# Lower prices for VectorE's operations in the planner that hands out the steps of two transforms between matmuls

## The chip, the cores and the metric

One Trainium2 chip, one of its cores. The metric is the device time of one execution in microseconds (us). Engines: TensorE (PE), VectorE (DVE), ScalarE (ACT), GpSimd (POOL) and SyncE (SP, which only issues DMAs here).

## The reference

```python
def _A_ref(x, w_r, w_i):
    X = jnp.fft.rfft2(x, axes=(-2, -1))
    X = X * (w_r + 1j * w_i)
    return jnp.fft.irfft2(X, s=(S, D), axes=(-2, -1))

def _B_ref(x, w1, w2):
    h = _silu(jnp.einsum("bsd,df->bsf", x, w1))
    return jnp.einsum("bsf,fd->bsd", h, w2)

xn = _layernorm(x)
return x + _A_ref(xn, w_r, w_i) * _silu(_B_ref(xn, w1, w2))
```

x is 2048 rows of 1024, w1 is 1024 by 3584, w2 is 3584 by 1024, w_r and w_i are 2048 by 513; all are float32. So there are two big matmuls with a SiLU between them (the dense part), and beside them a two-dimensional transform, a product with a filter and the inverse transform (the spectral part), joined in the last line.

## The kernel before, in words

Every float32 operand of a matmul is split into a high and a low half of 16 bits, and each product is made by three matmuls (high by high, high by low, low by high). `high` (L251, on ACT) and `low` (L254, on DVE) make the halves.

The dense part sets the order. The first matmul, `mm1` (L456), has 112 tiles of 24 matmuls of 512 columns: four blocks c of 512 rows by 28 blocks f of 128 hidden columns. The second, `mm2` (L539 to L541), is done with seven products m of sums and differences in place of eight; for each of them there are eight tiles j, and each tile is done in two halves of 21 matmuls of 512 columns. I call such a half of 21 matmuls a **half-tile**. `acc` adds a tile's result to the running sums (L582 to L609), and `w2_gen` prepares the weights of the next product, one block per call (L251, L254, tile `w`). The last sums go through `final` and `finish_out` (L623, L624) to the output.

The spectral part runs in the gaps, as generators in the list `bg`, in this order: layer norm (`ln_gen`), the forward transform along the rows (`fd_gen`, four blocks), the transform along the columns with the filter (`f_gen`), a small exact treatment of the edge of the spectrum (`edge_gen`), and the inverse (`i_gen`, four blocks c in the order 1, 3, 0, 2). Each `next` of a generator is one step: it issues some instructions on all engines and yields. All engines work their instructions off in the order of issue, so the order of the steps is the order on each engine.

`f_gen` has 16 turns u. A turn is four steps:

- step 1: `high_z(u-1)` (ACT L981), then on DVE `xb`, `xd` (L1004, L1005) and four operations of `radix4` (L238 to L241): 6 DVE operations, 2048 elements per partition in all.
- step 2: `low_z(u-1)` (L986) and the products with the filter (L1019, L1020): 3 operations, 3072 elements. Every fourth turn it also sets up the stores of `zq` to DRAM (`zd`, L990); `zq` has one buffer, so the next block of four waits for these stores.
- step 3: `mat(u+1)` on PE, 36 matmuls (L954 to L956), then on DVE L1032, L1033, L1036, L1037: 4 operations, 2048 elements.
- step 4: a copy on ACT (L975), the operations on `Z` (L1055): 8 on DVE with 896 elements, 4 on POOL.

After the last turn, `edge_gen` copies edge values on POOL (L1078 to L1081, behind POOL's share of the last `Z`), multiplies them by permutations on PE (`eps`, L1085 to L1087), and calculates on POOL.

In each block, `i_gen` has four matmul groups `iu` (L1204 or L1212) with the DVE work `post` (L1220 and on) and `split` (L1283, L1284), then four groups `mat2` (`id`, L1294) with the DVE work `bfly` (L1307 to L1341). `fx`, `iu`, `id` and `eps` take their PSUM tiles from one pool of two buffers; the result of group p leaves its buffer at L1308 of `bfly(p)`.

The planner is `work` (L1447). `meter` is called with every instruction as it is issued and keeps two clocks: for PE 0.4215e-3 us per column of output, for DVE a fixed price per operation and a price per element of the largest operand per partition. `work` is called once after each tile of `mm1` (but the first four) and after each half-tile of `mm2`. It gives one step to the weights (`wq`), lifts the DVE clock to at least the PE clock less 1.0, and then hands out up to three steps of `bg`, as long as the DVE clock is at most 1.0 (`LEAD`) ahead of the PE clock; a step that yields `PAUSE` ends it. In the last four tiles of `mm1` nothing is handed out (`hold`). 15 tiles before the end of `mm1` what is left of the forward transform is finished at once, and `f_gen` begins behind it.

Of the kernel before, what the change touches and what calls it, by code (L numbers as in the profile page):

```python
# [127 lines left out]
def spectral_ffn(ctx, tc, x, w_r, w_i, w1, w2, ca, kc, ci, tw, pm, out):  # L128
# [80 lines left out]

    clock = {"pe": 0.0, "dve": 0.0}  # L210

    COST = {"DVE": ("dve", 0.12, 1.05e-3), "PE": ("pe", 0.0, 0.4215e-3)}

    def meter(inst):

        name, fixed, each = COST.get(str(inst.engine).split(".")[-1], (None, 0, 0))
        rows = [math.prod(n for _, n in a.ap[1:]) for a in (*inst.outs, *(inst.ins if name == "dve" else ())) if hasattr(a, "bass_ap")]
# [1407 lines left out]
```

## Time and profile before

| | us |
|---|---|
| median of 3 runs (lowest, highest) | 1235.48 (1234.14, 1237.49) |
| the profiled execution's own time | 1235.84 |
| its span in the trace | 1234.1 |
| PE busy in the span | 1220.7 |
| DVE busy in the span | 999.0 |
| first `mm1` matmul to last `mm1` matmul | 19.3 to 636.3 |
| `mm2` | 636.5 to 1229.2 |

The span is the time from the first to the last instruction in the trace; 1.74 us of the execution lie outside it. A busy time is the time in which at least one instruction of the engine was under way. Matmuls overlap, so the busy time of PE does not say that it was at its peak; the distance between the starts of matmuls does. Idle time is put down to what ended it.

### The profile page before, as it was taken

What the parts mean: (1) busy time and instruction counts of PE and PEld (TensorE: products, weight loads), DVE (VectorE), ACT (ScalarE), POOL (GpSimd) and SP (SyncE); (2) the same over time, 40 slices, a digit from 0 to 9 for tenths busy, and PEclk for the clock granted to TensorE, in tenths of its full rate; (3) what the DMA queues carried; (4) which work ended last, traced back from release to release, by engine and by line L of the source; (5) the groups of instructions that cost most, each with busy time, mean ns of one, the idle gap of its engine ahead of it and who ended that gap; (6) DMA issues with size and microseconds to landing.
All of it is one profiled execution on the core that took longest, in us unless ns stands there. A gap on an engine that the chain in (4) does not pass through costs nothing.

```text
span 1234.1 us, 19097 instructions
## 1 busy us (share of the span) xinstructions
PE 1220.7 (99%) x7033; PEld 625.2 (51%) x7033; DVE 999.0 (81%) x1970; ACT 467.6 (38%) x614; POOL 117.3 (10%) x245
## 2 busy tenths in 40 slices
PE   8999999999999999999999999999999999999998
PEld 5545445444544454445545555554455555555545
DVE  7687988899798898896969899985186678798886
ACT  4865344333554565444433222122032222243212
POOL 2330000001000000010001121114111111000000
PEclk9999999999999999999999999999999999999999
DMA  7487476655758898759898999997989999998576
GB/s 253 134 172 187 135 224 201 185 152 161 223 172 237 276 283 242 217 177 279 207 283 224 283 259 198 276 256 246 293 207 278 286 289 331 315 332 325 200 261 260
DMA packets 271102, 293.67 MB, mean 238 GB/s; under 512 B 40096, under 2 KB 198816, under 8 KB 270624
## 3 DMA queue, kind: packets, MB, share of 16 engines
q1 hardware_dynamic: 250992, 233.66, 65.7%
q10 hardware_dynamic: 15984, 51.45, 12.0%
q0 software_dynamic: 4032, 7.34, 3.5%
q8 instruction: 55, 0.90, 0.3%
q14 instruction: 39, 0.32, 0.1%
HBM read 185.95 MB, written 102.25 MB: 234 GB/s over the span
## 4 chain that ended last, share of the span: by engine, by line
PE 75%; DVE 11%; DMA 9%; issue 2%; ACT 1%; SPq 0%; POOL 0%; DVEq 0%; ACTq 0%; POOLq 0%
PE pa L456 45%; PE pb L539 8%; PE pb L541 8%; PE pb L540 8%; DVE Z L1055 2%; DMA wq<-in_A_w_i_dram 2%; DMA sd<-s 2%; PE id L1294 2%; DMA zd<-zq 1%; DMA ht<-hd_sum_d 1%; DVE T L1020 1%; DVE w L254 1%; PE iu L1204 1%; ACT xp L709 1%; PE iu L1212 1%
## 5 line engine op out<-in xcount | busy, mean ns | idle before, releaser
L456 PE MATMUL pa<-xnT,w 128*128 128x512 f16 x2688 | 585.2, 379 | 1.1 <-ACT w L251 0.7
L456 PEld LDWEIGHTS <-w 128*128 128x128 f16 x2688 | 262.2, 98 | 311.6 <-DVE w L254 1.3
L539 PE MATMUL pb<-w,ht 128*128 128x512 f16 (+2 forms) x812 | 300.4, 372 | 0.0
L540 PE MATMUL pb<-w,ht 128*128 128x512 f16 (+2 forms) x812 | 300.4, 372 | 0.0
L541 PE MATMUL pb<-w,ht 128*128 128x512 f16 (+2 forms) x812 | 300.3, 372 | 0.0
L541 PEld LDWEIGHTS <-ht 128*128 128x128 f16 x812 | 79.4, 98 | 91.0
L539 PEld LDWEIGHTS <-ht 128*128 128x128 f16 x812 | 79.5, 98 | 86.7
L540 PEld LDWEIGHTS <-ht 128*128 128x128 f16 x812 | 79.4, 98 | 86.7
L465 ACT ACTIVATE h<-pa,s 128x512 f32<-128x512 f32 x112 | 75.5, 678 | 122.9 <-PE pa L456 111.0
L251 ACT ACTIVATE w<-jr,sc 128x512 f16<-128x512 f32 x98 | 68.1, 713 | 77.8 <-PE pb L541 22.1
L254 DVE SCALAR_TENSOR_TENSOR w<-jr,sc,w 128x512 f16<-128x512 f32 x98 | 71.1, 744 | 2.1 <-ACT w L251 2.1
L254 DVE SCALAR_TENSOR_TENSOR hoone<-h,hs,hoone 128x2048 f16<-128x2048 f32 x28 | 65.6, 2344 | 7.9 <-ACT hoone L251 7.9
L251 ACT ACTIVATE hoone<-h,hs 128x2048 f16<-128x2048 f32 x28 | 56.0, 1998 | 36.5 <-DVE h L499 24.3
L251 ACT ACTIVATE hosum<-hr,hs 128x1536 f16<-128x1536 f32 x28 | 44.1, 1574 | 64.1 <-DVE hr L495 26.8
L981 ACT ACTIVATE zq<-Z,zs 128x1024 f16<-128x1024 f32 x16 | 18.4, 1149 | 103.9 <-DVE Z L1055 57.0
L494 DVE TENSOR_TENSOR hr<-h 128x1024 f32<-128x1024 f32 x28 | 34.2, 1221 | 24.4 <-ACT h L465 24.3
L254 DVE SCALAR_TENSOR_TENSOR hosum<-hr,hs,hosum 128x1536 f16<-128x1536 f32 x28 | 50.7, 1812 | 3.1 <-ACT hosum L251 3.1
L251 ACT ACTIVATE w<-w1r,rs 128x1024 f16<-128x1024 f32 x28 | 31.9, 1144 | 47.0 <-DVE w L254 31.8
L274 DVE TENSOR_REDUCE m<-w1r 128x1 f32<-128x1024 f32 x28 | 33.8, 1210 | 16.1 <-DMA w1r<-in_B_w_dram 16.1
L632 ACT ACTIVATE pl<-pl,c 128x512 f32<-128x512 f32 (+2 forms) x28 | 17.6, 657 | 70.1 <-DVE pl L608 41.6
L954 PE MATMUL fx<-vq,kq 128*128 128x256 f16 x192 | 43.2, 273 | 0.0
L955 PE MATMUL fx<-vq,kq 128*128 128x128 f16 x192 | 42.0, 219 | 0.0
(219 smaller groups left out, 1524.8 us busy)
## 6 DMA issues: line engine op xcount, KB each, us to landing
w1r<-in_B_w_dram SPq DMA_DIRECT2D x28, 512.0 KB, 6.2
hd_sum<-hosum SPq DMA_DIRECT2D x56, 256.0 KB, 2.9
hd_one<-hoone SPq DMA_DIRECT2D x56, 256.0 KB, 3.7
hd_dif<-hoone SPq DMA_DIRECT2D x56, 256.0 KB, 3.2
w2m<-in_B_w_dram SPq DMA_DIRECT2D x28, 512.0 KB, 5.2
ht<-hd_dif ACTq DMA_DIRECT2D x32, 448.0 KB, 6.3
jr<-in_B_w_dram SPq DMA_DIRECT2D x56, 256.0 KB, 6.8
ht<-hd_sum ACTq DMA_DIRECT2D x32, 448.0 KB, 6.4
```

The costliest lines, as they stand in the source:

```text
L251: nc.scalar.activation(hi, raw, AF.Copy, scale=scale)
L254: nc.vector.scalar_tensor_tensor(lo, raw, scale, hi, op0=OP.mult, op1=OP.subtract)
L274: nc.vector.tensor_reduce(m1[:, i:i + 1], raw[i], axis=AX.XY, op=OP.max, apply_absolute_value=True)
L456: nc.tensor.matmul(ps, w[:, wh, d], xt[:, xh, d], start=(n == 0), stop=(n == 23))
L465: nc.scalar.activation(hq[:, 2 * (c % 2) + f % 2], ps, AF.Silu, scale=s1[:, f:f + 1])
L494: tt(sums[:, 0:2], hq[:, 0::2], hq[:, 1::2], op=OP.subtract)
L539: nc.tensor.matmul(ps, hh[:, 0], w[:, 0], start=first, stop=False)
L540: nc.tensor.matmul(ps, hh[:, 0], w[:, 1], start=False, stop=False)
L541: nc.tensor.matmul(ps, hh[:, 1], w[:, 0], start=False, stop=last)
L954: nc.tensor.matmul(o, k[:, c, kh, 1], v[:, c, vh], start=(n == 0), stop=False)
L955: nc.tensor.matmul(ps[:, c, 0], k[:, c, kh, 2], v[:, c, vh, 128:256], start=False, stop=False)
L1055: eng.tensor_tensor(Z[:, ns, pos], x0[:, :, ls], x1[:, :, ls], op=o_)
```

## The change

One line of numbers. The price of a DVE operation in the planner's clock goes from 0.12 us and 1.05 ns per element to 0.07 us and 1.0417 ns per element. No instruction is added or removed by hand; the steps are the same, and the planner decides anew after which tile each is issued.

```diff
     clock = {"pe": 0.0, "dve": 0.0}
 
-    COST = {"DVE": ("dve", 0.12, 1.05e-3), "PE": ("pe", 0.0, 0.4215e-3)}
+    COST = {"DVE": ("dve", 0.07, 1.0417e-3), "PE": ("pe", 0.0, 0.4215e-3)}
 
     def meter(inst):
```

## The prediction

> **What bounds the kernel now.** I read the page first, for the engines' shares.
>
> ```profile
> span 1234.1 us, 19097 instructions
> ...
> PE 1220.7 (99%) x7033; PEld 625.2 (51%) x7033; DVE 999.0 (81%) x1970; ACT 467.6 (38%) x614; POOL 117.3 (10%) x245
> ...
> PE   8999999999999999999999999999999999999998
> PEclk9999999999999999999999999999999999999999
> ```
>
> TensorE is busy in every slice at full clock. So the change can win only what TensorE still waits. Second view: its waits (total, times, longest).
>
> ```profile
> PE tp L718 <- ACT x L709: 3.0, 3, 2.0
> PE iu L1212 <- DVE ub L1221: 1.7, 1, 1.7
> PE fa L782 <- DVE xnT L726: 1.5, 1, 1.5
> PE spin L1465 <- POOL mhalf L1479: 1.0, 1, 1.0
> ```
>
> All but the second belong to the start (layer norm, warming matmuls, the first transform tile), which the planner hardly orders. So at most some 2 us can be won; what can be lost is open, since each wait that a new order puts before a matmul is paid in full. About 0.3%, or 3.7 us, is what a measurement of this kernel can tell from no change.
>
> Third, where VectorE has room (windows: PE, PEld, DVE, ACT and POOL busy; then clock and DMA share).
>
> ```profile
> 100.00:550.00 450.00, 450.00 (x2361) 216.56 (x2359) 394.10 (x804) 210.28 (x248) 20.23 (x38) 1.00 0.69 203
> 650.00:700.00 50.00, 50.00 (x329) 27.86 (x326) 44.12 (x78) 15.31 (x23) 6.24 (x13) 1.00 0.95 267
> 700.00:750.00 50.00, 50.00 (x328) 27.97 (x327) 49.79 (x93) 12.02 (x17) 10.87 (x17) 1.00 0.97 245
> 750.00:800.00 50.00, 50.00 (x305) 26.63 (x303) 49.86 (x95) 10.35 (x14) 7.64 (x17) 1.00 0.96 232
> ```
>
> From 700 to 800 us, in f_gen, VectorE has no room at all: 49.8 of 50. A lower price makes the planner hand out steps sooner, and there VectorE can't do them sooner. That is the stage to work out.
>
> **f_gen, by the planner's arithmetic.** A half-tile is 21 matmuls of 512 columns: 21 x 512 x 0.4215e-3 = 4.53. The group of step 3 counts 6144 columns, 2.59. The prices of steps 1 to 4 (6, 3, 4, 8 operations; 2048, 3072, 2048, 896 elements) are 2.87, 3.59, 2.63, 1.90 before and 2.55, 3.41, 2.41, 1.49 after; a turn costs 10.99 before and 9.87 after. An operation of 512 elements on the dense side costs 0.66 before, 0.60 after.
>
> After the change, from the lowest lead, -1.00: step 3 gives -1.00 + 2.41 - 2.59 = -1.18, step 4 +0.32, step 1 +2.87: three steps, over the limit. Next half-tile: 2.87 - 4.53 + 0.60 = -1.06, lifted to -1.00, and step 2 gives 2.41. Next: 2.41 - 4.53 + 1.21 = -0.91, and step 3 is due again. A turn closes in exactly **two half-tiles**, each time. Before, the same walk gives -0.96, 0.94, 3.81; then -0.06 or 0.60 (one or two dense operations), step 2 to 3.53 or 4.18; then -0.35 or 0.31, and steps 3 and 4 end at 1.59 or 2.25, over the limit, so that step 1 slips and the turn takes three. Mostly it alternates. The trace, from the group of u=4 to edge_gen's matmuls:
>
> ```profile
> L540 PE MATMUL pb<-w,ht 128*128 128x512 f16 x225 | 85.3, 379 | 0.0
> ...
> L954 PE MATMUL fx<-vq,kq 128*128 128x256 f16 x144 | 32.4, 273 | 0.0
> ```
>
> 225 matmuls of L540 are 32 half-tiles (7 each), and 144 / 12 = 12 groups. The last two half-tiles have no group, so 12 turns took 30 half-tiles, 2.5 each; 24 after the change. This window is 666.3 to 843.1, 176.8 us, so a group takes (176.8 - 32 x 4.53) / 12 = 2.65 of TensorE.
>
> What VectorE needs for these 12 turns, from one L1032 (668.18) to the twelfth after it (838.46):
>
> ```profile
> 668.18:838.46 170.28, 170.28 (x1062) 92.08 (x1059) 156.01 (x287) 40.23 (x56) 26.60 (x51) 1.00 0.95 254
> ```
> ```profile
> L254 DVE SCALAR_TENSOR_TENSOR w<-jr,sc,w 128x512 f16<-128x512 f32 x26 | 19.1, 742 | 0.4 <-ACT w L251 0.4
> ...
> L986 DVE SCALAR_TENSOR_TENSOR zq<-Z,zs,zq 128x1024 f16<-128x1024 f32 x12 | 15.3, 1276 | 13.3 <-ACT zq L981 13.3
> ...
> L585 DVE TENSOR_TENSOR c<-kept,pb 128x512 f32<-128x512 f32 x8 | 5.4, 674 | 0.0
> ...
> L588 DVE TENSOR_TENSOR kept<-kept,pb 128x512 f32<-128x512 f32 x1 | 0.7, 676 | 0.0
> ```
>
> The time that an operation takes from VectorE is the distance to the next start, shorter than its own duration:
>
> ```profile
> 741.95 0.67 DVE L1004 TENSOR_TENSOR xb<-fx,xc 128x512 f32<-128x512 f32 x1
> 742.55 0.67 DVE L1005 TENSOR_TENSOR xd<-fx,xc 128x512 f32<-128x512 f32 x1
> ...
> 744.49 0.67 DVE L585 TENSOR_TENSOR c<-kept,pb 128x512 f32<-128x512 f32 x1
> 745.09 0.73 DVE L254 SCALAR_TENSOR_TENSOR w<-jr,sc,w 128x512 f16<-128x512 f32 x1
> 745.75 1.27 DVE L986 SCALAR_TENSOR_TENSOR zq<-Z,zs,zq 128x1024 f16<-128x1024 f32 x1
> ...
> 755.04 0.67 DVE L1004 TENSOR_TENSOR xb<-fx,xc 128x512 f32<-128x512 f32 x1
> ```
>
> So L585 takes 0.60 and L254 0.66. The turn of 13.09 us (741.95 to 755.04) holds one L585 and two L254, which leaves 13.09 - 0.60 - 1.32 = 11.17. The twelve turns agree: (156.0 - 26 x 0.66 - 9 x 0.60) / 12 = 11.1. **The old price of a turn, 10.99, was nearly what it takes; the new one, 9.87, is 1.3 us too low.** The rest of the 170.3 is 13.3 of waiting at L986 for ACT's zq, which waits for the stores of the one buffer.
>
> Can TensorE run ahead of VectorE without loss? For some microseconds; but at the end of f_gen it must meet it:
>
> ```profile
> 838.46 0.68 DVE L1032 TENSOR_TENSOR T<-T,T 128x512 f32<-128x512 f32 x1
> ...
> 841.45 1.05 POOL L1055 TENSOR_TENSOR Z<-yd 128x32 f32<-128x32 f32 x2
> ...
> 842.44 0.38 POOL L1078 COPY edge<-xsv 128x24 f32<-128x24 f32 x1
> ...
> 843.20 0.30 PE L1085 MATMUL eps<-edge,perm 128*128 128x24 f32 x2
> ...
> 845.03 0.18 POOL L1081 COPY edge<-xsv 128x6 f32<-128x6 f32 x1
> ...
> 845.44 0.37 PE L1087 MATMUL eps<-edge,perm 128*128 128x8 f32 x2
> ```
>
> The edge matmuls read POOL's copies, these stand behind POOL's part of the last Z, and that behind VectorE's last turn. TensorE arrives at 843.20 and is held until the last copies, at 845: before, the two meet almost exactly. After, TensorE has six half-tiles fewer in this stretch, 6 x 4.53 = 27.2 us. VectorE has fewer dense operations: (26 + 9) / 32 = 1.1 per half-tile, some 6 fewer, 3.8 us. **So TensorE waits 27.2 - 3.8 = 23.4 us** in this stretch, wherever it shows (at the edge matmuls, or earlier at late ht tiles, whose loads are issued by ACT behind its wait for Z, or at the PSUM pool). The six half-tiles are done later; they are not saved. The 13.3 us of zq waits may change with the traffic: gone, the loss is 10; half as long again, 30. I take the row itself, since DMA stays over 0.9 busy.
>
> **i_gen.** The trace has two groups of mat2 at once, then one per half-tile:
>
> ```profile
> 937.30 3.05 PE id L1294 x48
> 944.88 1.53 PE id L1294 x24
> ```
> ```profile
> 940.29 0.67 DVE L1308 TENSOR_TENSOR sk<-id,sc 128x504 f32<-128x504 f32 x1
> ```
>
> A group counts 3489 columns, 1.47; bfly has 14 operations with 3312 elements, 5.16 before, 4.43 after. From -1.00 two groups and one bfly come to +1.22 before, which stops; after, to +0.49, and a third group goes out at once. It needs the buffer of the first, free at 940.29 + 0.67 = 940.96, while TensorE would be ready at 937.14 + 3.05 = 940.2: a wait of 0.8 in each of four blocks, **3.2**. The 1.7 at L1212 should go. Shorter spacing of the iu groups (post and split cost 6.6 before, 5.7 after) takes VectorE's slack ahead of mat2(0): 0 to 4 in all; I take 1, near the 1.7 of the one such wait shown. Net +2.5.
>
> **The first matmul.** There 804 operations become 0.05 x 804 = 40 us cheaper, so the forward transform ends many tiles sooner. It wins nothing, since f_gen's start is tied to a tile. VectorE, 394 of 450 busy, fills up while it lasts; TensorE waits for nothing there in before. I take 0; the bound is 3, twice the 1.5 of L782. The tail is the same instructions: 0.
>
> **Sum**: 23.4 + 2.5 = 25.9; span 1234.1 + 25.9 = 1260.0; with the 1.74 outside it 1261.7. The profiled run is 0.36 above the median, so **1261.4** for a median.
>
> **Rivals.**
>
> 1. *The backlog is absorbed* (not slower): each operation costs only its start-to-start distance, VectorE follows, and TensorE meets it at the edge matmuls as before. It decides at a turn of two half-tiles and a group, 2 x 4.53 + 2.65 = 11.7, less 1.4 of dense operations: VectorE would need a turn of 10.3. For it: the 0.60 between L1004 and L1005, which is the new price to the digit. Against it: 11.1 in every turn seen, without gaps. Then only the net of +1.5 from i_gen's third group against L1212 stays: 1237; with that also hidden, 1234.
> 2. *The zq waits shrink* (slower, by less): fewer ht loads per us let the stores land sooner. All 13.3 gone: 1248; with i_gen at nothing, 1245. For it: L986's whole wait hangs on stores. Against it: the DMA share of 0.95 and more.
> 3. *The clock drops in long waits*: if TensorE stands for many microseconds at a time, it may restart slowly, as at the start:
>
> ```profile
> 0.99 5.75 PE L1465 MATMUL spin<-ones 128*128 128x256 f16 x35 [0.99 <-POOL mhalf L1479]
> ```
>
> 35 spins of 256 columns at half of the 0.216 of 512 columns would be 3.8; they took 5.75, so a slow start costs about 2. Only the last of f_gen's waits counts, since VectorE sets the time up to there; with one more in i_gen, +2 to +4: 1264 to 1266. [...]
> 4. *The planner's order is other than I walked it* (turns of 2 and 3 again): near 1240. The margins of the walk, 0.68 at step 4's limit, speak against it.
>
> **Chances.** Forecast, 1250 to 1263: 0.56. Rival 3, up to 1270: 0.13. Rival 2, 1242 to 1250: 0.14. Rival 4: 0.05, of which 0.02 within 0.3% of 1235.48 (up to 1239.2). Rival 1: 0.12, of which 0.03 below 1231.8, 0.07 within 0.3% and 0.02 above. That makes 0.03 faster, 0.09 same and 0.88 slower. The range 1242 to 1270 leaves out rivals 1 and 4 and a little of each end.
>
> **What would show it.** Right: 26 half-tiles (182 matmuls of L540) between the group of u=4 and the edge matmuls; VectorE at 11.1 per turn; new TensorE waits of some 23 us in all at L1085, at pb for ht, or at fx, all before the edge matmuls' end; four waits of 0.8 at L1294. Wrong: no wait over 2 us in f_gen (rival 1); L986's 13.3 near nothing (2); matmuls 0.43 apart behind a wait (3); waits of 5 us or more in the first matmul or in i_gen, which I put at next to nothing.

## The result, and the profile after

The changed kernel takes 1273.82 us (median of 5 runs, 1269.65 to 1277.31) beside 1236.48 for the kernel before (5 runs, 1234.14 to 1239.02): a ratio of 1.0301, 95% interval 1.0281 to 1.0320, 37.3 us slower. The profiled execution took 1273.82 us, its span is 1272.0, 37.9 more than before. The forecast was 1261.4, the range ended at 1270.

The page of the changed kernel first: the span, the busy times, and two rows of the 40 slices.

```profile
span 1272.0 us, 19114 instructions
...
PE 1230.9 (97%) x7033; PEld 629.0 (49%) x7033; DVE 999.0 (79%) x1970; ACT 466.3 (37%) x614; POOL 112.2 (9%) x245
...
PE   8999999999999999999999989699999999899998
...
PEclk9999999999999999999999999889999999899999
```

VectorE is as busy as before, to the tenth of a us: the same 1970 operations, no faster for their new price. TensorE now has gaps, and its busy time has *grown* by 10.2 us with the same 7033 matmuls. Part of that is the clock, whose row dips behind the gaps. TensorE's waits (total, times, longest):

```profile
PE eps L1085 <- POOL edge L1078: 13.6, 1, 13.6
PE id L1294 <- DVE sk L1308: 7.8, 4, 5.5
PE fx L954 <- DMA vq<-vd: 3.4, 3, 1.6
PE pb L539 <- DMA ht<-hd_dif: 2.3, 1, 2.3
PE tp L718 <- ACT x L709: 2.3, 3, 1.6
PE fa L782 <- ACT L L792: 1.5, 1, 1.5
PE fa L782 <- DVE xnT L726: 1.5, 1, 1.5
PE pa L456 <- ACT h L465: 1.0, 1, 1.0
```

The largest stands at the edge matmuls, as foretold. New as well: waits for vq and ht inside f_gen, one wait at `id` that is seven times as long as its three sisters, and 2.5 us in the first matmul. The 1.7 us at L1212 are gone.

**f_gen.** The half-tiles between the group of u=4 (655.4) and the edge matmuls, and VectorE's L1032 over the same twelve turns, its operations and its windows:

```profile
L540 PE MATMUL pb<-w,ht 128*128 128x512 f16 x182 | 69.7, 383 | 0.0
```
```profile
L1032 DVE TENSOR_TENSOR T<-T,T x13: 672/682/693, 664.3 to 823.2; 128x512 f32<-128x512 f32 x13
```
```profile
664.30:823.20 158.90, 143.61 (x914) 77.96 (x912) 152.04 (x281) 39.54 (x57) 27.07 (x51) 0.97 0.91 241
```
```profile
L254 DVE SCALAR_TENSOR_TENSOR w<-jr,sc,w 128x512 f16<-128x512 f32 x24 | 17.5, 742 | 0.0
L986 DVE SCALAR_TENSOR_TENSOR zq<-Z,zs,zq 128x1024 f16<-128x1024 f32 x12 | 15.3, 1276 | 6.4 <-ACT zq L981 6.4
L585 DVE TENSOR_TENSOR c<-kept,pb 128x512 f32<-128x512 f32 x5 | 3.4, 675 | 0.0
```

182 matmuls are 26 half-tiles; VectorE's turn is (152.04 - 24 x 0.66 - 5 x 0.60) / 12 = 11.1 us. Both are the predicted numbers. Where the turn's 1.3 us above the new price sit can be read from the kernel before: in the turn that the prediction shows, the eight operations on Z start with

```profile
752.40 0.91 DVE L1055 TENSOR_TENSOR Z<-yb 128x128 f32<-128x128 f32 x2
```

and end with the start of the next L1004 at 755.04. They take 2.64 us, where the new price counts 1.49 and the old one 1.90. Two other numbers are not as predicted: the waits at L986 are 6.4, not 13.3, and VectorE's L1032 starts 664.3 - 655.4 = 8.9 us behind the group of u=4, where before it was 668.2 - 666.3 = 1.9.

To measure the loss without the idle times of a view, I take the stretch from the group of u=4 to the 42nd `pb` matmul behind the edge matmuls, less 0.216 us for each `pb` matmul in it. In the changed kernel these two starts are

```profile
655.43 0.27 PE L954 MATMUL fx<-vq,kq 128*128 128x256 f16 x1
...
842.27 0.38 PE L541 MATMUL pb<-w,ht 128*128 128x512 f16 x1
```

and 842.27 - 655.43 - (546 + 41) x 0.216 = 60.05; the kernel before has 34.14 by the same sum (854.51 - 666.36 - 713 x 0.216). I call this number the **excess** of f_gen: +25.9 by the change. Most of the 34.1 is the twelve groups' own work, 12 x 2.65 = 31.8. The excess is the measure for the experiments below. It is read from one execution of each kernel, and two executions of one and the same program (e4_edge and e13_ht below) gave 46.2 and 51.8, so a difference of 5 us between two kernels with such waits says little by itself.

**The clock.** Windows of the changed kernel around the wait (PE, PEld, DVE, ACT, POOL busy; then granted clock, DMA share, GB/s):

```profile
810.00:815.00 5.00, 4.29 (x20) 1.76 (x18) 4.97 (x12) 0.00 (x0) 1.87 (x4) 1.00 0.68 179
815.00:820.00 5.00, 0.00 (x0) 0.00 (x0) 5.00 (x11) 2.99 (x4) 0.00 (x0) 0.81 0.60 197
820.00:825.00 5.00, 0.00 (x0) 0.00 (x0) 4.96 (x7) 0.00 (x0) 0.00 (x0) 0.50 0.29 60
825.00:830.00 5.00, 2.11 (x10) 2.11 (x11) 4.08 (x11) 0.83 (x1) 4.51 (x16) 0.50 0.24 86
830.00:835.00 5.00, 5.00 (x17) 2.92 (x18) 2.54 (x3) 0.57 (x2) 2.65 (x12) 0.50 0.94 307
835.00:840.00 5.00, 5.00 (x24) 2.28 (x23) 0.76 (x2) 0.33 (x1) 4.04 (x22) 0.98 1.04 407
```

The clock goes to half some 4 us into the wait and stays there for the edge matmuls and for 3.4 us of full work behind them; VectorE is busy throughout, so it is VectorE that is waited for.

**i_gen's long wait.** A timeline of ScalarE and POOL ahead of it, and TensorE's `id` groups with the first `pb` matmul behind them:

```profile
1090.57 0.86 POOL L416 DMA_DIRECT2D jr<-in_B_w_dram  x1 [10.66 <-DMA jr<-in_B_w_dram]
...
1099.67 0.72 ACT L251 ACTIVATE w<-jr,sc 128x512 f16<-128x512 f32 x1 [8.88 <-DMA jr<-in_B_w_dram]
1100.30 0.57 ACT L1303 ACTIVATE sc<-id 128x504 f32<-128x504 f32 x1
```
```profile
1093.71 3.21 PE L1294 MATMUL id<-cis,us 128*128 128x130 f16 x48
1102.46 3.07 PE L1294 MATMUL id<-cis,us 128*128 128x130 f16 x24 [5.54 <-DVE sk L1308]
1105.33 0.63 PE L539 MATMUL pb<-w,ht 128*128 128x512 f16 x1
```

The third group waits for VectorE's L1308, that for ScalarE's L1303, and L1303 stands in ScalarE's queue behind L251, which waits 8.9 us for a weight block whose sum POOL issued at 1090.57. Three queues stand in a row, each in order. Behind the wait the granted clock is 0.50 from 1101.4 to 1108.2 us: from the wait's end to the 30th `pb` matmul TensorE takes 12.09 us, and 9.31 in each of the three other blocks. So the half clock adds 2.8 us here.

### The profile page after: what moved, and what is told of

Same layout as the page of the kernel before. It is cut to its first block, busy times and chain, and to the rows that moved or that the text cites. A ratio compares the mean times of both kernels' runs of the same rounds, so it can differ in the third digit from the quotient of the medians.

```text
span 1272.0 us, 19114 instructions
## 1 busy us (share of the span) xinstructions
PE 1230.9 (97%) x7033; PEld 629.0 (49%) x7033; DVE 999.0 (79%) x1970; ACT 466.3 (37%) x614; POOL 112.2 (9%) x245
## 4 chain that ended last, share of the span: by engine, by line
PE 65%; DVE 15%; DMA 12%; issue 3%; ACT 3%; SPq 2%; POOL 0%; ACTq 0%; DVEq 0%; POOLq 0%
PE pa L456 35%; PE pb L539 8%; PE pb L540 8%; PE pb L541 8%; DMA jr<-in_B_w_dram 3%; DMA zd<-zq 2%; DVE Z L1055 2%; DMA jr<-ws 2%; DVE w L254 1%; DMA wq<-in_A_w_r_dram 1%; PE id L1294 1%; DVE T L1020 1%; DVE zq L986 1%; DMA hd_one<-hoone 1%; PE iu L1204 1%
## 5 line engine op out<-in xcount | busy, mean ns | idle before, releaser
L456 PE MATMUL pa<-xnT,w 128*128 128x512 f16 x2688 | 585.5, 379 | 2.2 <-ACT h L465 1.0
L456 PEld LDWEIGHTS <-w 128*128 128x128 f16 x2688 | 262.1, 98 | 312.3 <-DVE w L254 1.3
L251 ACT ACTIVATE w<-jr,sc 128x512 f16<-128x512 f32 x98 | 68.0, 712 | 63.8 <-DMA jr<-in_B_w_dram 31.0
L251 ACT ACTIVATE hoone<-h,hs 128x2048 f16<-128x2048 f32 x28 | 55.9, 1996 | 59.5 <-DVE h L499 28.3
L251 ACT ACTIVATE hosum<-hr,hs 128x1536 f16<-128x1536 f32 x28 | 44.0, 1572 | 90.5 <-DVE hr L495 67.5
L254 DVE SCALAR_TENSOR_TENSOR hoone<-h,hs,hoone 128x2048 f16<-128x2048 f32 x28 | 65.6, 2343 | 11.1 <-ACT hoone L251 11.1
L494 DVE TENSOR_TENSOR hr<-h 128x1024 f32<-128x1024 f32 x28 | 34.1, 1218 | 20.4 <-ACT h L465 20.3
L251 ACT ACTIVATE w<-w1r,rs 128x1024 f16<-128x1024 f32 x28 | 31.9, 1142 | 41.9 <-DVE w L254 17.5
```

The lines of the kernel that those rows point to most:

```text
L251: nc.scalar.activation(hi, raw, AF.Copy, scale=scale)
L254: nc.vector.scalar_tensor_tensor(lo, raw, scale, hi, op0=OP.mult, op1=OP.subtract)
L456: nc.tensor.matmul(ps, w[:, wh, d], xt[:, xh, d], start=(n == 0), stop=(n == 23))
L494: tt(sums[:, 0:2], hq[:, 0::2], hq[:, 1::2], op=OP.subtract)
```

## The experiments

Times stand beside the kernel before run on the same chip (medians 1234.8 to 1237.4); "over before" is the difference of these medians. In kernels with added lines the line numbers are up to five higher.

### One stage at a time

```diff
+    PRICE = {True: ("dve", 0.07, 1.0417e-3), False: ("dve", 0.12, 1.05e-3)}
+    stage = ["fd"]
...
+        COST["DVE"] = PRICE[stage[0] in ("f",)]
...
+        stage[0] = "f"
```

The last line stands at f_gen's start, one with "i" at i_gen's. e2_i has ("i",) in the test, e3_fd ("fd",).

> The finer prices stand only while the steps of f_gen are handed out; the layer norm, the forward transform and i_gen keep the old ones. Theory: the loss is made at one place, the edge matmuls (L1085), which the finer prices set 26 half-tiles behind group u=4 instead of 32, while VectorE's turns still take 11.1 us; that cost 24.3 us after, with another 1.6 us of matmuls at half clock behind the wait. So this part alone gives 24 to 28 us over before, 1260 to 1264 us, with one wait of 12 to 18 us at L1085 and matmuls 0.43 us apart behind it. Rival (the loss is spread over all stages, and f_gen's wait is only where it happens to end): less than 15 us over before, under 1251 us.

1263.68 us, ratio 1.0210 (1.0189 to 1.0231): 27.1 over before. The waits:

```profile
PE pb L542 <- DMA ht<-hd_dif: 10.5, 3, 6.3
PE eps L1089 <- POOL edge L1082: 6.8, 1, 6.8
```

The time is as the theory has it, the place only in part: 10.5 us are waited ahead, for ht, and only 6.8 at the edge matmuls. The excess of f_gen is 64.0 (+29.9).

> The finer prices stand only while the steps of i_gen are handed out. Theory: a third mat2 group is placed in each of the four blocks, and each waits about 0.9 us for L1308; that is 4 x 0.9 = 3.7 us, less 1.9 us of waits that went. The one wait of 5.7 us of the changed kernel (4.8 more than its three sisters) came from a weight load that landed late in front of ScalarE's L1303, and need not come again. So 2 to 5 us over before without it (1238 to 1241 us), 7 to 9 us with it and its half-clock matmuls. Rival (the third group always meets such a load): 15 us or more over before. Rival (i_gen costs nothing, its waits would be there anyway): within 1 us of before.

1245.74 us, ratio 1.0087 (1.0058 to 1.0115): 9.2 over before. Four waits at `id`, 6.7 in all, one of 3.2. That one again came behind a weight block that POOL had issued at 1049.90: ScalarE waited 6.8 us for it at its L251, with L1303 next in the queue. A wait of 5.0 in e7 below came in the same way (8.7 us at L251). Of the twelve kernels here with a third group six have such a wait (2.9 to 5.8 us), and in all six L251 had waited 3.4 to 8.9 us for a block, with the copy L1303 next in the queue. The other six have none over 1.9 us, so the rival's "always" is too much.

> The finer prices stand only ahead of f_gen, for the layer norm and the forward transform. Theory: the two new waits of 1.65 and 1.18 us in the first matmul, 2.6 us after, and f_gen as before, so 1 to 4 us over before, 1237 to 1240 us. Rival (handing the forward transform out 18 half-tiles early starts f_gen early too, with a longer lag of VectorE, and a good part of the wait at L1085 comes from there): 8 us or more over before, with a wait at L1085.

1238.71 us, ratio 1.0015 (1.0003 to 1.0028): 2.1 over before; the excess of f_gen 33.6, as before. Starting f_gen's lag from here (the rival) is out. **The three stages give 27.1 + 9.2 + 2.1 = 38.4; the whole change 37.3.** They add up.

### i_gen: the third group

```diff
-            yield 3.4 if p else 0.3
+            yield PAUSE if p == 1 else 3.4 if p else 0.3
```

This stands on e2_i.

> The kernel with the finer prices in i_gen alone (9.2 us over before: one wait of 0.92 us at L1299 in most blocks, one of 3.3 us, and waits of 0.7, 1.1 and 2.2 us in the last), with a pause behind the second mat2 group of each block, so that the third group can't be placed in the same work call. Theory: the third group is the cost of i_gen, so nearly all of the 9 us goes: within 3 us of before, no waits at the id matmuls. Rival (i_gen's later steps being drawn forward cost by themselves, through VectorE and the loads): 5 us or more over before.

1234.39 us, ratio 0.9977 (0.9960 to 0.9993), 11 us below e2_i; no wait at `id` is left. Since this is as fast as any kernel here, it ran once more.

> The finer prices in i_gen alone with a pause behind the second mat2 group, once more (1234.39 us in its first runs, 0.9977 of before, 0.9960 to 0.9993). Theory: the 1.9 us of waits at L1212 that before has are gone and nothing is put in their place, so 1 to 3 us faster than before: ratio 0.9975 to 0.9990. Rival (chance of the runs): ratio 1.000 or above.

1234.38 us, ratio 0.9984 (0.9969 to 0.9999). So the third group is the whole cost of i_gen, and drawing the steps forward costs nothing without it. This is the fastest version found, by about 0.2%, less than the 0.3% that I take a measurement to tell.

### f_gen: how far the edge matmuls stand

| kernel | half-tiles from u=4 to the edge matmuls | excess of f_gen, us | over before, us |
|---|---|---|---|
| before | 32 | 34.1 | 0 |
| after | 26 | 60.1 | 37.3 |
| e1_f | 26 | 64.0 | 27.1 |
| e10_mid (0.10 per operation) | 31 | 43.4 | 11.4 |
| e9_slope (only the slope) | 33 | 36.5 | 2.6 |
| e7_turn (+1.1 per turn) | 39 | 33.6 | 14.8 |
| e4_edge | 31 | 46.2 | 27.2 |
| e12_late | 31 | 48.9 | 26.3 |

```diff
             zs_[u] = Z.rearrange("m n l i -> m (n l) i")
+            clock["dve"] += 1.1
             yield 2.9
```

That is e7_turn, on the changed kernel. e10_mid is the changed kernel with 0.10 in the place of 0.07, e9_slope with 0.12.

> The changed kernel, with 1.1 us added to VectorE's price for each turn of f_gen, which then costs 10.97 us where VectorE takes 11.1. By the hand-out this closes a turn in 3 half-tiles each, and sets the edge matmuls 39 half-tiles behind group u=4 (32 before, 26 after). Theory: f_gen's 24 to 26 us go whole; the first matmul's 2.6 and i_gen's 7 to 9 stay: 1245 to 1250 us, no wait at L1085. Rival (the room in f_gen is taken from behind it: i_gen now starts six half-tiles later than before and the last finals wait for it): 1258 us or more.

1251.68 us, ratio 1.0120 (1.0092 to 1.0149), 1.7 above the range given. No wait at L1085, an excess below before's: f_gen's loss is gone whole with a turn priced at what it takes. i_gen cost more than I allowed, with one wait of 5.0 at `id`: by the same sum, the stretch from the 42nd `pb` matmul behind the edge matmuls to the last one took 14.9 us more than before, and 9.3 more in the changed kernel. So 5.5 of the 26.5 us that f_gen got back were lost again behind it; whether i_gen's later start is the reason was not tried.

> A fixed price of 0.10 us per operation instead of 0.07 (after) or 0.12 (before), everywhere, with the new slope. By the hand-out the edge matmuls stand 31 half-tiles behind group u=4 (26 after, 32 before), and the third mat2 group is still placed in i_gen. Theory: the loss of f_gen is a matter of that distance: five half-tiles are 22.6 us, which takes the wait of 13.8 us and most of the 8 us of waits ahead of it; i_gen's 6 to 9 us stay. 1241 to 1249 us, no wait over 3 us at L1085. Rival (the loss grows evenly with the price taken off, 0.02 of 0.05): 15 us over before, 1251 us or more, with a wait at L1085.

1248.29 us, ratio 1.0100 (1.0063 to 1.0137), within the range; 2.7 us waited at the edge matmuls and 3.2 for ht. With 31 half-tiles, one fewer than before, the excess is still 9.2 above before. So the distance is most of it, and not all.

> Only the price per element is the finer one (1.0417 ns instead of 1.05); the fixed part stays at 0.12 us. Over VectorE's 1970 operations and 769,022 elements of a partition the slope takes 769,022 x 0.0083 ns = 6.4 us off the whole price and the fixed part 1970 x 0.05 us = 98.5 us. Theory: the change is all in the fixed part; here the edge matmuls keep their distance from group u=4 within a half-tile or two and no third mat2 group is placed: within 3 us of before. Rival (any price below the old one makes the steps come early enough to wait): 6 us or more over before.

1239.50 us, ratio 1.0020 (1.0006 to 1.0034): 2.6 over before, one wait of 2.7 for ht. The fixed part is the change.

```diff
             g.tensor_copy(r0[:, n, 1:4], xv[:, n, 0, 3:0:-1])
-        yield 1
+        for _ in range(5):
+            yield PAUSE
         ps = pt.tile([128, 1024], F32, name="eps", tag="ft")
...
-                add(bg, switch(B, open_i, 6, lag=2))
+                add(bg, switch(B, open_i, 2, lag=2))
```

On the changed kernel. e12_late has the first part alone.

> The changed kernel with its finer prices, but the edge matmuls (L1085) stand five half-tiles (22.6 us) later in the order, and i_gen starts one half-tile later. Theory: the wait of 13.8 us goes with the half clock around it (3.9 us for the edge matmuls and the switch instead of about 1.5, and 1.6 us behind them), so about 18 us under the changed kernel, 1254 to 1258 us; the remaining 18 to 20 us over before are the six half-tiles that f_gen's turns lost, as waits elsewhere or as matmuls left without transform work beside them, plus i_gen and the first matmul. If the place of the edge matmuls is the whole loss of f_gen, the time is 1245 to 1250 us. Rival (VectorE is behind by the same amount at every later meeting, so the wait only moves to the switch or to the start of i_gen): 1268 us or more.

1263.72 us, ratio 1.0212 (1.0190 to 1.0235). **A miss**: 10.1 gained, not 18. The wait at L1085 is gone, but the excess is 12.1 above before:

```profile
PE pb L539 <- DMA ht<-hd_dif: 6.3, 3, 3.3
PE iu L1205 <- DMA kk<-in_kc_dram: 4.4, 1, 4.4
PE id L1295 <- DVE sk L1309: 3.0, 4, 0.8
```

> As the kernel with the later edge matmuls, but with the six pauses of the switch kept, so that i_gen starts five half-tiles later than in the changed kernel. In the kernel with two pauses, 4.4 us were waited at i_gen's first matmul (L1205) for its kk load. Theory: that wait came from the switch's lead that was cut with the pauses, so it goes: 4 us or more below that kernel's 1263.7, 1256 to 1260 us; f_gen's waits for ht and fx (about 11 us) stay. Rival (the wait for kk is VectorE's lag arriving at i_gen, whatever the lead): 1262 us or more.

1263.20 us, ratio 1.0204 (1.0180 to 1.0228). Again a miss, and in the range of the rival: the wait for kk is gone, as the theory had it, and the time is not, beyond 0.9 us. The excess is 48.9, 7.8 us are waited for ht and 3.7 for vq. So turns of two half-tiles cost 12 to 18 us wherever the edge matmuls stand (e4_edge, e12_late, and e13_ht below, against the 34.1 of before). What paces them?

### What is left: queue or transfers

> As the kernel with the later edge matmuls (1263.7 us), with the loads of ht issued from SP's queue instead of ScalarE's. In that kernel TensorE waited 6.3 us for ht in three waits, and each of the late loads was issued right behind a ScalarE operation (L981) that had waited about 10 us for VectorE's Z or for a transfer. Theory: VectorE's lag reaches the second matmul by that queue; with the loads past it, the 6.3 us go and 2.5 to 7 us are gained: 1257 to 1261 us. Rival (VectorE paces f_gen and a wait avoided here is made at the next matmul of the transform, fx or eps): within 2 us of that kernel. Rival (SP's queue is itself held by what it waits for, and ht comes later still): slower by 3 us or more.

1261.91 us, ratio 1.0211 (1.0180 to 1.0242). This run tells nothing on the queue: the edit changed a default of `load_h`, and the call behind the half-tiles (L1557) names ScalarE's queue itself, so all loads stayed where they were. It is e4_edge once more, and shows the scatter of one program: 2 us between the medians, and an excess of 51.8 where e4_edge had 46.2. Mended, on e12_late, and on the kernel before:

```diff
-                    load_h(*seq[n + 2], k, nc.scalar)
+                    load_h(*seq[n + 2], k, nc.sync)
```

> The kernel with the later edge matmuls and all six pauses of the switch (1263.2 us; from group u=4 to the second half-tile behind the edge matmuls it takes 48.9 us beside the second matmul's own time, 34.1 before, 60.1 after), with the loads of ht that follow each half-tile issued from SP's queue. Theory: the four waits for ht (0.5, 2.7, 0.6 and 4.6 us by the trace's order, 7.8 in the view of waits) and the half clock behind the last (2.3) are made in ScalarE's queue; without them 6 to 10 us less, 1253 to 1257 us. The two waits for vq's load (1.9 and 2.0) stay. Rival (VectorE paces the stage, the time is waited for at fx or eps instead): within 2 us of 1263.2. Rival (SP's queue is held too): 1266 us or more.

1261.09 us, ratio 1.0201 (1.0184 to 1.0217): **the theory falls** as the main cause. 7.0 us are still waited for ht. By the starts of the matmuls the late waits, past 810 us, went from 5.2 (0.65 + 4.56) to 2.5; those at 750 to 765 us grew from 3.2 to 5.1.

> The kernel before with the same move of the loads of ht to SP's queue, prices untouched. Theory: before has no wait for ht, so nothing is to be gained; within 3 us of 1236.5, and e15's gain is then VectorE's lag taken off the queue and not a better queue as such. Rival (SP's queue is the better one in any case): 3 us or more faster. Rival (SP's queue is full and the loads come late): 3 us or more slower, and e15 would understate what the mechanism costs.

1235.65 us, ratio 0.9991 (0.9977 to 1.0005): the queue as such makes no difference.

Next the transfers: 12 of 16 pairs of wq loads left out, the factors of every fourth turn used in their place.

```diff
             q, j = u // 4, u % 4
+            if j:
+                return
...
-            wr, wi = B["w"].pop((u, 0)), B["w"].pop((u, 1))
+            wr, wi = B["w"][u - j, 0], B["w"][u - j, 1]
```

> The kernel with the later edge matmuls and all pauses of the switch (1263.2 us), loading wq only in every fourth turn of f_gen; the three turns between reuse it, so that 12 of 16 pairs of loads (256 KB each, 6.3 of the 40.6 MB that the changed kernel moves from 655 to 830 us) and the right factors of these turns are left out. VectorE's operations stay the same. Theory: f_gen's turns, drawn into fewer half-tiles, now ask more of the DMA engines than they move in the time, and TensorE waits for ht and vq; with 15% of the bytes gone these waits (11.5 us by the view of waits, and 2.3 of half clock) fall to 4 or less: 1250 to 1257 us. Rival (VectorE paces f_gen, ht and vq wait for buffers that it frees): within 2 us of 1263.2.

1256.21 us, ratio 1.0161 (1.0131 to 1.0191): 21.5 over before, where e12_late was 26.3. Two windows and the loads of ht at 740 to 765 us (count, size, median us to landing), e12_late first:

```profile
680.00:705.00 25.00, 25.00 (x179) 14.64 (x176) 21.34 (x41) 7.91 (x12) 2.85 (x7) 1.00 0.92 269
730.00:755.00 25.00, 22.84 (x154) 12.61 (x152) 23.87 (x45) 6.30 (x9) 4.45 (x9) 1.00 0.98 222
```
```profile
ht<-hd_dif ACTq DMA_DIRECT2D x5, 448.0 KB, 11.4
```

and e18_late_wq:

```profile
680.00:705.00 25.00, 25.00 (x175) 14.45 (x173) 24.93 (x46) 7.90 (x12) 2.85 (x6) 1.00 0.67 226
730.00:755.00 25.00, 25.00 (x165) 13.98 (x164) 23.28 (x44) 6.07 (x9) 3.62 (x8) 1.00 0.59 191
```
```profile
ht<-hd_dif ACTq DMA_DIRECT2D x4, 448.0 KB, 6.1
```

With the DMA engines at 0.59 instead of 0.98 a load lands in 6.1 us instead of 11.4, and TensorE waits for nothing in mid-stage. The excess falls from 48.9 to 42.8, which alone would be within the scatter, and the intervals of the two ratios just overlap; e20_after_wq below, with the same loads left out, is clear of the changed kernel. What stays is 6.0 us for ht in two waits at 809 and 823 us, with the DMA engines half idle: there ScalarE had waited 10.2 and 10.7 us ahead of its write of zq (for Z, and behind the edge copies) with the loads queued behind it. So **both** are at work: slow landing in mid-stage, ScalarE's queue at its end. e15 took half of the second and left the first.

The slow landing is not new, though. The kernel before, in the same windows:

```profile
730.00:755.00 25.00, 25.00 (x162) 13.71 (x160) 24.93 (x47) 6.54 (x11) 7.15 (x9) 1.00 1.00 300
```
```profile
ht<-hd_dif ACTq DMA_DIRECT2D x5, 448.0 KB, 11.2
```

Its DMA engines are as full and its loads as slow, and TensorE waits for none of them, because they are issued sooner: those used from 740 to 765 us were issued 17 to 23 us ahead of their first matmul, in e12_late 9 to 17, and the two that were late there 9.0 and 13.2 us ahead. With the loads on SP's queue (e15) the two late ones were issued 10.8 and 13.0 us ahead, hardly sooner. By these traces the change took from the loads the time ahead of their use, and not the speed of the transfers.

> The kernel before with the same 12 pairs of wq loads left out. Theory: it has no wait for a transfer in f_gen, so the loads cost it nothing: within 2 us of 1236.5. Rival (the transfers slow the stage in some other way, by the ports of the memory or the queues): 3 us or more faster, and the gain of the other two runs is to be read less this.

1235.88 us, ratio 1.0002 (0.9986 to 1.0019). With 2.5 half-tiles per turn the loads come early enough either way; the wq loads cost the kernel before nothing.

> The changed kernel itself with the same 12 pairs of wq loads left out. Theory: here VectorE's 16 turns end at the same time whether TensorE waits early or at the edge matmuls, so what is saved in waits for ht and vq is waited at L1085: the wait there grows to 16 to 22 us, the time stays within 4 us of 1273.8. Rival (the transfers also hold VectorE up, by late vq and wq): 1262 us or less, with a wait at L1085 of no more than 14 us.

1265.54 us, ratio 1.0242 (1.0205 to 1.0279): 30.8 over before where the changed kernel was 37.3, and the intervals do not overlap. Neither theory nor rival had it. The wait at L1085 is 15.0, near the theory's lower end, but the whole stage ends earlier. VectorE at the low half of zq from 650 to 850 us, changed kernel and e20_after_wq:

```profile
L986 DVE SCALAR_TENSOR_TENSOR zq<-Z,zs,zq 128x1024 f16<-128x1024 f32 x14 | 17.9, 1277 | 7.7 <-ACT zq L981 7.7
```
```profile
L988 DVE SCALAR_TENSOR_TENSOR zq<-Z,zs,zq 128x1024 f16<-128x1024 f32 x14 | 17.9, 1276 | 2.1 <-ACT zq L983 2.1
```

Its idle time there went from 7.7 to 2.1 us: the transfers hold VectorE too, through the stores of the one zq buffer (in the changed kernel the last store of a block landed at 688.5 us, and ScalarE wrote zq at 688.7). Of f_gen's 25.9 us of added excess, 7.5 go with these loads (60.05 to 52.54).

### The clock

Added matmuls of 256 columns (0.109 us each) on the ones tile, ahead of the edge matmuls, 100 in e5_spin, 128 in e14_spin128:

```diff
+        spin(100)
         ps = pt.tile([128, 1024], F32, name="eps", tag="ft")
```

> The changed kernel, with 100 added matmuls of 256 columns on the ones tile (0.109 us each at full clock by the start-up rows, 10.9 us in all) right in front of the edge matmuls, so that TensorE works while it waits for POOL's edge copies; nothing of the computation is left out. The wait itself can't get shorter, only the clock is kept up. Theory: the half clock of 818 to 835 us in the changed kernel costs 1.6 us behind the edge matmuls and about 2 us at them, so 3 to 4 us less than the changed kernel: 1269 to 1272 us, and the matmuls behind the edge group 0.216 us apart instead of 0.43. Rival (the clock costs nothing here, because what is done at half speed is itself waiting): the same as the changed kernel within 1 us. Rival (the added matmuls do not fit into the wait): slower.

1269.62 us, ratio 1.0261 (1.0229 to 1.0292). The number fits the theory, its reason does not: the added matmuls ended 2.9 us before the edge copies came, and the clock fell all the same, for less long:

```profile
825.00:830.00 5.00, 2.85 (x18) 2.76 (x19) 3.72 (x11) 1.15 (x1) 4.04 (x16) 0.89 0.20 40
830.00:835.00 5.00, 5.00 (x14) 1.85 (x14) 2.04 (x3) 0.25 (x1) 4.17 (x19) 0.50 0.97 321
```

The excess is 60.8, no gain in f_gen. What was gained here lies elsewhere (i_gen's long wait was 2.9 instead of 5.5).

> As the kernel with 100 added matmuls in front of the edge matmuls, with 128 (14.0 us). With 100 of them TensorE still waited 2.9 us for the edge copies behind them, and the clock fell to half for some 6 us there. Nothing of the computation is left out. Theory: with the wait filled to its end the clock stays up through the edge matmuls, and the two half-clock stretches behind a wait that is left (each 1.2 to 2.7 us) go at this place: 1 to 4 us below the changed kernel's 1273.8, 1269 to 1273 us, with pb matmuls 0.216 us apart behind the edge group. Rival (the clock falls with the small edge matmuls themselves, which keep TensorE little busy for 3 us, whatever runs ahead): half clock for 3 us or more behind them again, and the same time as with 100.

1268.80 us, ratio 1.0248 (1.0210 to 1.0286). The same windows:

```profile
825.00:830.00 5.00, 4.91 (x43) 4.29 (x40) 3.90 (x11) 1.01 (x1) 4.54 (x16) 1.00 0.20 70
830.00:835.00 5.00, 5.00 (x26) 2.38 (x27) 2.64 (x4) 0.39 (x2) 3.83 (x16) 1.00 0.87 231
```

Full clock through the edge group, though it has the same small matmuls. From the first edge matmul to the 42nd `pb` matmul behind takes 11.29 us (827.73 to 839.02); the changed kernel took 14.38 (827.89 to 842.27), the kernel before 11.31 (843.20 to 854.51). **The half clock costs 3.1 us at this place.** (f_gen's whole excess, 57.8, is 2.2 below the changed kernel's, since the stretch ahead of the edge matmuls was 0.8 us longer in this execution.)

Why did some waits halve the clock and others not? The length of the wait does not tell: the clock fell behind one of 2.3 us in the changed kernel and stayed up through one of 3.2 in e2_i. Windows of 3.41 us around the first wait, then the second:

```profile
746.41:749.82 3.41, 1.25 (x6) 0.39 (x4) 3.41 (x10) 0.73 (x1) 1.39 (x4) 1.00 1.11 227
749.82:753.24 3.42, 3.25 (x8) 1.19 (x9) 3.42 (x7) 1.65 (x3) 0.00 (x0) 0.50 0.93 63
```
```profile
1055.86:1059.27 3.41, 1.86 (x30) 1.65 (x27) 0.00 (x0) 1.17 (x4) 0.00 (x0) 1.00 1.06 360
1059.27:1062.69 3.42, 1.80 (x26) 1.68 (x27) 3.15 (x7) 0.76 (x4) 0.00 (x0) 1.00 1.08 444
```

The first two windows are cut along the changed kernel's own record of the clock. It is at half from 749.82 to 753.24, from 818.09 to 835.16 and from 1101.40 to 1108.22 us, that is for 3.41, 17.07 and 6.83 us, or 1, 5 and 2 times 3.413; the 64.85 and 266.24 us of full clock between are 19 and 78 times as much. The shorter wait left TensorE idle for 2.16 us (3.41 - 1.25) of one such step, and the clock fell at its end. The longer one was split over two windows of the same length, with 1.55 and 1.62 us idle, and the clock stayed at 1.00 in both. The steps ahead of the changed kernel's two other falls, from 814.68 and from 1097.98 us, were idle throughout; of its steps at full clock that no fall followed the idlest had 1.48 us (790.78 to 794.20), and 1.60 in the start (5.72 to 9.13). Where between 1.62 and 2.16 us a limit lies, if there is one, these windows do not show, and idle time alone does not decide: around the small edge matmuls of e6_two the clock fell with 0.70 us idle in 841 to 844 us and 0.32 in 844 to 847 (granted 0.90 in 844 to 847, 0.53 in 847 to 850).

## Why the prediction was too low

Direction, main place and main mechanism were right; the sum was 25.9 where 37.9 came. The step that failed most is the price of i_gen, +2.5 where 9.3 came. By its own steps:

- **The price is too low for f_gen's turn, and TensorE gets there six half-tiles early: right.** 26 half-tiles, 11.1 us per turn. Rival 4 (another order) is out, and so is rival 1 (the backlog absorbed).
- **"TensorE waits 27.2 - 3.8 = 23.4": the sum right, by two errors that cancelled.** The excess grew by 25.9, of which 3.1 are the clock: 22.8. But VectorE's twelve turns took 158.9 instead of 170.3 us, 11.4 less and not 3.8, since the waits at L986 were halved (rival 2, in part) and dense operations fell from 35 to 29, by 3.7 us; and VectorE was already 8.9 us behind at u=4, 7.0 more than before, which I had not asked. 27.2 - 11.4 + 7.0 = 22.8. The list of places where the waits could show was complete. That the total came out within 0.6 us is luck.
- **"Only the last of f_gen's waits counts" with +2 to +4 was a rival at 0.13, and it came true (rival 3).** It cost 3.1 at the edge group by e14 and 2.8 behind i_gen's long wait (12.09 - 9.31), 5.9 together and more than the rival allowed. It should have stood in the sum: the forecast itself had a wait of many microseconds at one place. The half speed could be read from the start of the kernel before, where spins of 256 columns stand 0.213 us apart up to 4.59 us and 0.109 behind that. In the changed kernel it did not take a long wait: 2.16 us of idle time in one step of 3.41 us, at 746.41, were followed by the half clock.
- **"i_gen, net +2.5": the step that failed most.** The third group was foreseen, four waits at L1294 too, and three of them were 0.76 long, as priced. The fourth was 5.5: the waits come to 7.8 - 1.7 = 6.1, with the 2.8 of half clock to 8.9. The whole stretch from the 42nd `pb` matmul behind the edge matmuls to the last one, less 0.216 per `pb` matmul, grew from 29.9 to 39.3, by 9.3, so 0.4 is left that was not told apart. I priced the wait by L1308's operations as they stood, and not by what stands ahead of them in ScalarE's queue, which is a load of the dense part. e2_i (9.2 over before) and e6_two (2.5 under before) show that the third group alone decides there; half of the kernels with it had short waits only, as priced, so whether a late block meets the third group differs from kernel to kernel.
- **"The first matmul: I take 0; the bound is 3": 2.7 came**, by the same sum up to the group of u=4 (58.54 before, 61.21 after), of which 2.5 are new waits (1.5 at L782, 1.0 at L456). e3_fd was 2.1 over before. The bound held, the value didn't: with the steps handed out sooner TensorE came to L782 ahead of ScalarE's L792.

22.8 + 3.1 + 9.3 + 2.7 = 37.9, the whole of what the span grew by. The range ended 3.8 us too low because each of the three small terms, the clock, i_gen and the first matmul, was put at its friendly end.

What the prediction didn't have at all is what e4 to e20 showed: had the edge matmuls stood later, 12 to 18 us would have stayed, since with turns of two half-tiles the loads of ht are issued closer to their use than with 2.5. What part of the rest of e18's excess (42.8 against 34.1) is VectorE's pace and what the queue was not tried by taking both away at once.

## What to carry to other kernels

A planner's price must be what an operation takes from its engine in the stage that is full, gaps, waits and small operations included, and not the distance between two operations in a good row: the price that is right for L1004, 0.60, leaves its turn 1.3 us too cheap, 1.15 of it in the eight small operations on Z. Where two in-order engines must meet at a fixed place, work out the lead of each at the start of the stretch too, since part of a loss can be there already (7.0 of 22.8 us here). And price a new wait by the longest thing that can stand in any of the queues behind it, with the clock's fall on top (2.8 and 3.1 us here).

## What the runs showed of the hardware

- The granted clock was 0.50 from about 818 to 835 us around a wait of 13.6 us; matmuls of 512 columns were then 0.43 us apart instead of 0.216, for 3.4 us of full work after the wait had ended. 100 small matmuls in the wait shortened the half-clock time from 17.07 to some 6.8 us (granted 0.89, 0.50 and 0.93 in the three windows of 5 us from 825 us) and gained nothing in f_gen (excess 60.8 beside 60.1); 128, which filled it, kept the clock at 1.00 and made the stretch behind it 3.1 us shorter.
- The length of a wait did not decide: half clock after 2.3 us (changed kernel, 750 us), none after 3.2 (e2_i) and 3.3 (e4_edge, 832 us). In the changed kernel the half-clock stretches lasted 3.41, 17.07 and 6.83 us, and the falls came behind steps of 3.41 us with 2.16, 3.41 and 3.41 us idle; 1.48 us (1.60 in the start) in one step was followed by none there, while in e6_two the clock fell with about 1.0 us idle in 841 to 847 us, around the small edge matmuls.
- Loads of 448 KB took 11.4 us to land with the 16 DMA engines 0.98 busy, and 6.1 in the same stage at 0.59. The rate only fell from 222 to 191 GB/s, so a seventh fewer bytes went with two fifths less busy time and with a time to landing that was nearly halved. A load that took 11.2 us cost nothing where it was issued 17 us or more ahead of its use (kernel before).
